# All of the first product by the seven-product scheme from the second block on, its last part moved behind the second product's first

## The chip, the core and the metric

The kernel runs on one core of one Trainium2 chip. A core has five engines that run beside each other, each in the order of its own queue: TensorE (PE; its weight loads are shown as PEld), VectorE (DVE), ScalarE (ACT), GpSimd (POOL) and SyncE (SP), which only starts transfers here. The metric is the device time of one launch in microseconds (us), taken as the median of several runs.

## The reference

Two stages follow each other. The first is a decayed linear attention (retention) over 768 tokens, for 4 batches and 8 heads of width 64; the second is a two-layer feed-forward with a Mish activation.

```python
for t in range(S):                                  # S = 768
    state = gamma * state + outer(k[:, :, t], v[:, :, t])
    y[:, :, t] = (1 / sqrt(64)) * q[:, :, t] @ state
x = y.transpose(0, 2, 1, 3).reshape(3072, 512)
h = x @ w_in                                        # 512 x 2048
g = h * tanh(softplus(h))                           # Mish
out = g @ w_out                                     # 2048 x 512
```

## The kernel before

The 3072 tokens are cut into 24 chunks of 128, and these into 11 blocks: block 0 has four chunks, blocks 1 to 10 have two each. For a block, the attention gives `xt` (the block's tokens of x, turned, FP16), the first product gives `g` through Mish, and the second product gives 256 rows of the output. In each block the attention of the next block runs in between: `scores` (queries by keys of a chunk), `mask` on VectorE, `y_two` (the attention's output for two chunks, and `outer_two`, the state's increments), then the copy to `xt`.

In a block after block 0 the second product (`seven`) is computed by the Strassen-Winograd scheme: the matrices are cut in 2 by 2 parts, and seven half-size products take the place of eight, at the price of sums before and after. Eight matmuls of 128x256 make one such product. The sums of `g` are written to `gsum` (s1 and s2 by `sums_a`, s3 by `sums_b`, s4 by `sums_c`), those of the weights to `tmat` once at the start (`weight_sums`).

The first product (`g1_seven`) is split before the change. The columns of w_in come as four slices of 512. Slices 0 and 2 go by seven products of eight 128x128 matmuls (`mm`, line 671), with `win_sums` giving the weight sums `wsum` and `x_sums` the token sums `xsum`. Slices 1 and 3 go plainly (`plain`, line 695): four pieces of eight 128x256 matmuls, each read straight from PSUM by a Mish on ScalarE (line 702). In the seven-product half three partial results are copied out of PSUM by ScalarE (`snap`, line 678), three sums PSUM + copy are formed by VectorE (`plus`, line 688), and four Mish follow (line 682).

PSUM has eight banks here: four for `mm` tiles of one bank (pool `mmps`), and two tiles of two banks each (pool `atps`, tag "at") that scores, `y_two` and the state increments share. A tile that needs a bank waits until the last reader of its earlier tenant is done.

The order is written out by hand: every engine executes its instructions in the order in which the code issues them, and the dictionaries of `steps_of` and `steps_of_first` say which work of the attention, the sums and the transfers is issued between which products. `gate(x)` is a one-element copy on GpSimd that makes GpSimd's queue wait for x. `sum_next` adds a state increment on VectorE, `decay_next` scales the state on GpSimd. Block 1 (`FIRST`) has its own dictionary; it also finishes block 0 (`last_ended`). In block 0, `cast_win` and `cast_wout` turn the loaded weights to FP16, and the list `late` holds sums of weights that `some_late` takes off one by one.

Of the kernel before, what the change touches and what calls it, by code (L numbers as in the profile page):

```python
# [16 lines left out]
def kernel(  # L17
# [165 lines left out]
    def cast_win(s, half, eng):  # L183
        src = wtmps["in", s]
        t = cpool.tile([P, NBP, TB // 2], FP16, name=f"win{s}_{half}")
        eng.tensor_copy(t, src[:, :, half * (TB // 2):(half + 1) * (TB // 2)])
        wins[s, half] = t
# [429 lines left out]
    def win_sums():  # L617
        wsums.append(wstage.tile([P, 4, NBP // 2, TB], FP16, name="wsum", tag="wt", bufs=4))
        sub, n = ALU.subtract, NBP // 2
        todo = []  # L620
        for half in range(2):
            s1, s2, s3, s4 = [
                wsums[0][:, i, :, half * (TB // 2):(half + 1) * (TB // 2)] for i in range(4)]
            a11, a12 = wins[0, half][:, :n], wins[0, half][:, n:]
            a21, a22 = wins[2, half][:, :n], wins[2, half][:, n:]
# [23 lines left out]
    def g1_seven(blk, steps):  # L649
# [4 lines left out]
        pb, px, pe = [mmps.tile([P, FPS, P], FP32, name="h_ps", tag="mm") for _ in range(3)]  # L654

        def a(i, j):
            return lambda f, d: win(2 * i, f, j * n + d)

        def s(i):
            return lambda f, d: wsums[0][:, i - 1, d, f * P:(f + 1) * P]  # L660

        def b(i, j):
# [5 lines left out]
        def mm(h_ps, w, x, first=False):  # L668
            for f in range(FPS):
                for d in range(n):  # L670
                    nc.tensor.matmul(  # L671
                        h_ps[:, f], w(f, d), x(d), start=first and f == 0 and d == 0,
                        stop=d == n - 1, skip_group_check=True)

        def snap(h_ps):
            x = hsnaps[0][:, nsnap[0] % 4].rearrange("p (f t) -> p f t", t=P)
            nsnap[0] += 1
            nc.scalar.copy(x, h_ps)  # L678
            return x

        def mish_of(i, j, h):
            nc.scalar.activation(  # L682
                gt[:, 2 * i * FPS:(2 * i + 1) * FPS, j * P:(j + 1) * P], h, AF.Mish,
                scale=inv_boost3)
# [6 lines left out]
        def plain(s, half):  # L691
            h_ps = mmps.tile([P, 2, 2 * P], FP32, name="h_ps", tag="mm")
            for j in range(2):
                for bp in range(NBP):
                    nc.tensor.matmul(  # L695
                        h_ps[:, j], win(s, 2 * half + j, bp), xt(blk, bp),
                        start=bp == 0, stop=bp == NBP - 1)
            return h_ps

        def mish_plain(s, half, h_ps):  # L700
            fb = s * FPS + 2 * half
            nc.scalar.activation(gt[:, fb:fb + 2], h_ps, AF.Mish, scale=inv_boost3)  # L702

# [494 lines left out]
```

## Time and profile before

| what | value |
|---|---|
| median of 3 runs | 198.35 us (197.97 to 198.6) |
| span of the profiled execution | 196.9 us, from its first to its last instruction |
| PE busy in the span | 190.0 us (97%) |
| DVE busy | 141.6 us (72%) |
| ACT busy | 105.5 us (54%) |
| POOL busy | 93.1 us (47%) |
| granted TensorE clock | 0.996 |
| the profiled execution's own time | not given beside its span |

The times of runs are those of whole executions; the profile gives of its own execution the span, and no other time. Between span and median lie 1.45 us, which are taken as what lies around the span. Rows of the chain and of the timeline give a start and a duration in us from the span's start. Matmuls are pipelined: in a row of several the last one's end is included, so that eight matmuls of 128x256 show as 1.04 us in the timeline but take 0.87 us of the chain.

### The profile page before, as it was taken

How to read it: one execution, taken by the hardware profiler on the slowest of the kernel's cores; microseconds unless marked ns; L12 is line 12 of the kernel's file. 1: busy time of each engine (PE TensorE's matmuls, PEld its weight loads, DVE VectorE, ACT ScalarE, POOL GpSimd, SP SyncE). 2: the span in 40 equal slices, each digit the busy share in tenths (PEclk: the TensorE clock that was granted, in tenths of full speed). 3: DMA queues.
4: the chain of work that ended last, by engine and by line, in shares of the span. 5: the costliest groups of instructions: out<-in, count | busy, mean ns of one | idle time of the engine just before them, and what ended most of it. 6: DMA issues, size and time to landing. Idle time of an engine off the chain costs nothing.

```text
span 196.9 us, 5965 instructions
## 1 busy us (share of the span) xinstructions
PE 190.0 (97%) x2482; PEld 158.8 (81%) x2482; DVE 141.6 (72%) x304; ACT 105.5 (54%) x193; POOL 93.1 (47%) x130
## 2 busy tenths in 40 slices
PE   6999999999999999999999999999999999999992
PEld 2557646876888988988988988988988988988991
DVE  3688699795897596597498596597497596596462
ACT  3364667443753753753753753753853843843930
POOL 4270214694848829918716818728626723110000
PEclk9999999999999999999999999999999999999998
DMA  5999999999999999997997994995988933101102
GB/s 170 350 375 405 405 407 225 331 174 83 137 214 237 232 205 230 197 130 199 179 212 97 227 172 103 153 217 119 176 201 128 189 65 110 55 0 72 41 27 80
DMA packets 95802, 36.06 MB, mean 183 GB/s; under 512 B 82592, under 2 KB 89376, under 8 KB 95776
## 3 DMA queue, kind: packets, MB, share of 16 engines
q1 hardware_dynamic: 74544, 33.04, 65.1%
q0 software_dynamic: 21088, 2.62, 22.3%
q8 instruction: 19, 0.31, 0.6%
q10 hardware_dynamic: 144, 0.03, 0.1%
q14 instruction: 7, 0.06, 0.1%
HBM read 27.30 MB, written 6.29 MB: 171 GB/s over the span
## 4 chain that ended last, share of the span: by engine, by line
PE 92%; DVE 2%; ACT 2%; issue 1%; POOL 0%; POOLq 0%; ACTq 0%
PE o_ps L777 32%; PE h_ps L695 17%; PE h_ps L671 15%; PE h_ps L556 5%; PE o_ps L1009 5%; PE y_ps L508 3%; PE at L439 3%; PE at L415 2%; PE o_ps L1067 2%; PE h_ps L866 2%; PE y_ps L499 1%; DVE am L291 1%; PE u_ps L454 1%; DVE st L315 1%; ACT hsnap L678 1%
## 5 line engine op out<-in xcount | busy, mean ns | idle before, releaser
L695 PE MATMUL h_ps<-xt,win 128*128 128x256 f16 x320 | 41.6, 273 | 0.0
L688 DVE TENSOR_TENSOR hsum<-h_ps,hsnap 128x512 f32<-128x512 f32 x30 | 19.8, 688 | 21.2 <-PE h_ps L671 19.1
L777 PEld LDWEIGHTS <-gsum 128*128 128x128 f16 x336 | 30.8, 98 | 4.1
L695 PEld LDWEIGHTS <-win 128*128 128x128 f16 x320 | 29.3, 98 | 3.6
L777 PE MATMUL o_ps<-tmat,gsum 128*128 128x256 f16 (+1 forms) x256 | 27.9, 266 | 0.0
L384 POOL DMA_DIRECT2D qk<-in_k_dram x36 | 27.8, 776 | 0.0
L777 PEld LDWEIGHTS <-g 128*128 128x128 f16 x256 | 23.7, 98 | 2.6
L682 ACT ACTIVATE g<-hsum 128x512 f16<-128x512 f32 x30 | 18.6, 630 | 11.7 <-DVE hsum L688 11.7
L445 DVE TENSOR_TENSOR am<-at,tri 128x1024 f16<-128x1024 f32 x20 | 24.2, 1216 | 0.2 <-PE at L439 0.2
L702 ACT ACTIVATE g<-h_ps 128x512 f16<-128x512 f32 x40 | 22.7, 599 | 2.4 <-PE h_ps L695 2.4
L397 POOL COPY gate<-gsum 128x1 f16<-128x1 f16 x12 | 2.6, 213 | 44.3 <-DVE gsum L743 36.8
L786 ACT COPY snap<-o_ps 128x256 f32<-128x256 f32 (+1 forms) x32 | 11.4, 359 | 21.7 <-PE o_ps L777 21.5
L389 POOL TENSOR_TENSOR v<-vf,qvs 128x512 f16<-128x512 f32 x20 | 23.0, 1153 | 0.0
L678 ACT COPY hsnap<-h_ps 128x512 f32<-128x512 f32 x30 | 16.4, 580 | 12.1 <-PE h_ps L671 12.1
L799 DVE TENSOR_TENSOR osb<-o_ps,snap 128x256 f32<-128x256 f32 (+1 forms) x31 | 12.7, 410 | 12.6 <-PE o_ps L777 11.5
L372 POOL TENSOR_TENSOR qk<-qf,qvs 128x512 f16<-128x512 f32 x20 | 21.7, 1086 | 0.0
L541 ACT CAST xt<-y_ps 128x1024 f16<-128x1024 f32 x10 | 10.1, 1012 | 19.3 <-PE y_ps L499 14.3
L671 PEld LDWEIGHTS <-wsum 128*128 128x128 f16 x320 | 19.6, 98 | 0.8 <-issue 0.3
L777 PE MATMUL o_ps<-wout,g 128*128 128x256 f16 (+1 forms) x168 | 19.3, 268 | 0.0
L671 PE MATMUL h_ps<-xsum,wsum 128*128 128x128 f16 x240 | 16.7, 219 | 0.2 <-ACT hsnap L678 0.2
L671 PEld LDWEIGHTS <-win 128*128 128x128 f16 x240 | 15.1, 98 | 0.7
L614 DVE TENSOR_TENSOR gsum<-g 128x256 f16<-128x256 f16 (+1 forms) x30 | 9.9, 331 | 3.8 <-ACT g L682 3.6
(126 smaller groups left out, 296.1 us busy)
## 6 DMA issues: line engine op xcount, KB each, us to landing
vf<-in_v_dram SPq DMA_DIRECT2D x24, 256.0 KB, 5.3
out_dram<-osb SPq DMA_DIRECT2D x22, 256.0 KB, 4.7
qf<-in_q_dram SPq DMA_DIRECT2D x20, 256.0 KB, 4.3
wi<-in_moe_w_in_dram SPq DMA_DIRECT2D x3, 1024.0 KB, 10.6
wt<-in_moe_w_out_dram SPq DMA_DIRECT2D x3, 1024.0 KB, 8.8
qk<-in_k_dram POOLq DMA_DIRECT2D x36, 64.0 KB, 4.4
qfirst<-in_q_dram SPq DMA_DIRECT2D x2, 512.0 KB, 4.4
kf<-in_k_dram SPq DMA_DIRECT2D x4, 256.0 KB, 5.0
```

Of the source, the lines that this page charges most:

```text
L372: nc.gpsimd.tensor_tensor(by_head(g, room16(g)[0]), by_head(0, loaded[g][0]), f.broadcast_to((P, 2, HP, D)), op=ALU.mult)
L384: nc.gpsimd.dma_start(room16(g)[1][:, x::2], src[:, HP * x:HP * x + HP])
L389: nc.gpsimd.tensor_tensor(room16(g)[2], loaded[g][2], vs.unsqueeze(2).broadcast_to((P, H, D)), op=ALU.mult)
L445: nc.vector.tensor_tensor(am, ats.pop(g), tri.unsqueeze(1).unsqueeze(1).broadcast_to((P, 2, HP, C)), op=ALU.mult)
L671: nc.tensor.matmul(h_ps[:, f], w(f, d), x(d), start=first and f == 0 and d == 0, stop=d == n - 1, skip_group_check=True)
L678: nc.scalar.copy(x, h_ps)
L682: nc.scalar.activation(gt[:, 2 * i * FPS:(2 * i + 1) * FPS, j * P:(j + 1) * P], h, AF.Mish, scale=inv_boost3)
L688: nc.vector.tensor_tensor(h, h_ps, x, op=ALU.add)
L695: nc.tensor.matmul(h_ps[:, j], win(s, 2 * half + j, bp), xt(blk, bp), start=bp == 0, stop=bp == NBP - 1)
L702: nc.scalar.activation(gt[:, fb:fb + 2], h_ps, AF.Mish, scale=inv_boost3)
L777: nc.tensor.matmul(t, x(f), w(f)[:, c], start=first and f == 0, stop=f == n - 1, skip_group_check=True)
L799: nc.vector.tensor_tensor(dst[:, c], t, plus[:, c], op=ALU.add)
```

## The change

`g1_seven` computes slices 1 and 3 by seven products as well. There are now two groups, g = 0 (slices 0 and 2) and g = 1 (slices 1 and 3), each of seven products of eight 128x128 matmuls; `plain` is gone. Group 1 has weight sums of its own (`win_sums(1)`, eight more VectorE operations in block 0). The cast of slice 3 of w_in moves from VectorE to ScalarE in block 0. Of the fourteen products of a block, thirteen stand in `g1_seven`; the last one of group 1 (`rest`) stands in `seven`, behind the second product's first product and the scores. A two-bank "at" tile (`both`) holds two of the eight PSUM tiles that the two groups need. One of the six copies out of PSUM, that of the fifth product of group 0, is made by VectorE. The sums of `g` are issued later: s1 and s2 in two parts of the size 128x512 (before: one of this size and two of 128x256), s3 behind the first mask and s4 behind the second. In `seven`, the products with `sm(1)` and `sm(2)` now come ahead of the one with `wouts` that completes the first. GpSimd's second gate of a block (`gate_s`, which waits for s4) stands in blocks 2 to 8 too, ahead of the casts of q and v and the loads of k that the block issues there; before it stood in block 1 alone. The remaining weight sums of w_out are made before block 1, not in it.

```diff
@@ cast_win
-        eng.tensor_copy(t, src[:, :, half * (TB // 2):(half + 1) * (TB // 2)])
+        src = src[:, :, half * (TB // 2):(half + 1) * (TB // 2)]
+        if eng is nc.scalar:
+            nc.scalar.copy(t, src)
+        else:
+            eng.tensor_copy(t, src)
...
@@ win_sums
-    def win_sums():
-        wsums.append(wstage.tile([P, 4, NBP // 2, TB], FP16, name="wsum", tag="wt", bufs=4))
+    def win_sums(a):
+        if a == 0:
+            t = wstage.tile([P, 4, n, TB], FP16, name="wsum", tag="wt", bufs=4)
+            wsums.append([t[:, i] for i in range(4)])
+        else:
+            wsums.append([
+                lpool.tile([P, n, TB], FP16, name="wsum", tag="kf", bufs=4) for _ in range(4)])
...
@@ g1_seven
-        pb, px, pe = [mmps.tile([P, FPS, P], FP32, name="h_ps", tag="mm") for _ in range(3)]
+        both = atps.tile([P, 2, FPS, P], FP32, name="h_ps", tag="at")
+        pb, px, pe, px1 = [
+            mmps.tile([P, FPS, P], FP32, name="h_ps", tag="mm") for _ in range(4)]
+        pb, px, pe = [pb, both[:, 0]], [px, px1], [pe, both[:, 1]]
...
-        mm(px, a(0, 0), b(0, 0), True)
-        m1 = snap(px)
-        step("p1")
-        mm(pb, a(0, 1), b(1, 0), True)
-        c11 = plus(pb, m1)
-        step("p2")
-        h0 = plain(1, 0)
-        mm(px, s(2), t(2))
-        mish_of(0, 0, c11)
-        u2 = snap(px)
-        mm(pe, s(1), t(1), True)
-        m5 = snap(pe)
-        mish_plain(1, 0, h0)
-        step("p6")
-        h1 = plain(3, 0)
...
+        def first_two(g):
+            mm(px, g, w(0, 0), x(0, 0), True)
+            m1[g] = snap(px[g])
+            mm(pb, g, w(0, 1), x(1, 0), True)
+        def second(g):
+            mm(px, g, s(2), t(2))
+            u2[g] = snap(px[g])
+        def fifth(g):
+            mm(pe, g, s(1), t(1), True)
+            m5[g] = snap(pe[g], g == 0)
+        first_two(0)
+        step("g1")
+        c0 = plus(pb[0], m1[0])
+        first_two(1)
+        mish_of(0, 0, 0, c0)
+        step("g2")
+        c1 = plus(pb[1], m1[1])
+        second(0)
+        mish_of(1, 0, 0, c1)
+        fifth(0)
+        step("g3")
+        second(1)
+        fifth(1)
+        mm(px, 0, s(3), t(3))
+        c22 = plus(px[0], m5[0])
+        mm(pe, 0, s(4), x(1, 1))
+        c12 = plus(pe[0], u2[0])
+        mish_of(0, 1, 1, c22)
+        mish_of(0, 0, 1, c12)
+        step("g4")
...
+        step("g5")
+        mm(px, 0, w(1, 1), t(4))
+        mish_of(0, 1, 0, px[0])
+        def rest():
+            mm(px, 1, w(1, 1), t(4))
+            mish_of(1, 1, 0, px[1])
@@ seven
-        pb, pe = [mmps.tile([P, hf], FP32, name="o_ps", tag="mm") for _ in range(2)]
         px = [mmps.tile([P, wide], FP32, name="o_ps", tag="mm") for _ in range(parts)]
+        pe = mmps.tile([P, hf], FP32, name="o_ps", tag="mm")
...
         mm(px, a(0, 0), b(0, 0), True)
         m1 = snap(px)
+        step("g7")
         step("m1")
+        rest()
+        pb = mmps.tile([P, hf], FP32, name="o_ps", tag="mm")
+        mm(pe, s(1), tm(1), True)
+        m5 = snap(pe)
+        step("m5")
+        mm(px, s(2), tm(2))
+        u2 = snap(px)
+        step("m6")
         mm(pb, a(0, 1), b(1, 0), True)
...
@@ first_block
-        late.extend(weight_sums(0) + weight_sums(1))
-        plan = {9: [(cast_wout, 0), (room_for_more,), (bring_first,)],
+        def more_sums():
+            late.extend(win_sums(1))
+            some_late(8)
+            late.extend(weight_sums(0) + weight_sums(1))
+        plan = {6: [(cast_win, NSL - 1, 0, nc.scalar)],
+                7: [(cast_win, NSL - 1, 1, nc.scalar), (more_sums,)],
+                9: [(cast_wout, 0), (room_for_more,), (bring_first,)],
@@ steps_of
+            "g1": [*then((gate_x, blk), (cast_q, a)), (sum_next, a - 3), (decay_next, a - 3),
+                   (cast_v, a), (bring_k, a + 1)],
+            "g2": [(store_due, 1), (turn_and_load, a)],
+            "g3": [(store_due, 2), (sum_next, a - 2)],
+            "g5": [(store_due, 3), (sums_a, blk, A)],
+            "g7": [(sums_a, blk, B)],
+            "m1": only((scores, a - 2), (scores, a - 1), (mask, a - 2)),
+            "m5": [(sums_b, blk), *only((gate_g, blk), (decay_next, a - 2))],
+            "m6": [*only((mask, a - 1)), (sums_c, blk), *then((gate_s, blk)),
+                   (cast_q, a + 1), (cast_v, a + 1), (bring_k, a + 2)],
+            "m2": [(turn_and_load, a + 1)],
...
@@ steps_of_first
-            "p1": [(last_ended.pop(),)],
-            "p2": [(gate_x, blk), (cast_q, a - 1), (bring_k, a), (sum_next, a - 2)],
+            "g1": [(last_ended.pop(),), (gate_x, blk), (cast_q, a - 1), (bring_k, a), (sum_next, a - 2)],
...
```

Three places show how the instructions stand now. The first is VectorE in block 0, from the last casts of slice 2 of w_in to the second slice of w_out; before (`win` and `wout` are cast weights, `wi` and `wt` the loaded ones, `wsum` the sums for the first product, `gsum` and `tmat` those for the second):

```order
L633 TENSOR_TENSOR wsum<-win_0_381,wsum 128x2x256
L186 COPY win_0_534<-wi 128x1024
L186 COPY win_1_536<-wi 128x1024
L633 TENSOR_TENSOR wsum<-win_1_527 128x2x256
L633 TENSOR_TENSOR wsum<-wsum,win_1_458 128x2x256
L633 TENSOR_TENSOR wsum<-win_1_458,win_1_527 128x2x256
L633 TENSOR_TENSOR wsum<-win_1_458,wsum 128x2x256
L194 COPY wout_574<-wt 128x2048
L591 TENSOR_TENSOR tmat<-wout_574 128x1024
L976 TENSOR_TENSOR gsum<-g 128x1024
L978 TENSOR_TENSOR gsum<-gsum,g 128x1024
L194 COPY wout_605<-wt 128x2048
```

The same place now, from the last sum of group 0's weights on:

```order
L643 TENSOR_TENSOR wsum<-win_1_458,wsum 128x2x256
L643 TENSOR_TENSOR wsum<-win_0_551 128x2x256
L643 TENSOR_TENSOR wsum<-wsum,win_0_499 128x2x256
L643 TENSOR_TENSOR wsum<-win_0_499,win_0_551 128x2x256
L643 TENSOR_TENSOR wsum<-win_0_499,wsum 128x2x256
L643 TENSOR_TENSOR wsum<-win_1_559 128x2x256
L643 TENSOR_TENSOR wsum<-wsum,win_1_501 128x2x256
L643 TENSOR_TENSOR wsum<-win_1_501,win_1_559 128x2x256
L643 TENSOR_TENSOR wsum<-win_1_501,wsum 128x2x256
L198 COPY wout_586<-wt 128x2048
L595 TENSOR_TENSOR tmat<-wout_586 128x1024
L1005 TENSOR_TENSOR gsum<-g 128x1024
```

Two casts of 128x1024 are gone from VectorE's queue there, and eight sums have come in ahead of the casts of w_out.

The second place is VectorE in a block in the middle, from the first sum PSUM + copy to the first mask; before:

```order
L688 TENSOR_TENSOR hsum<-h_ps,hsnap 128x512
L466 TENSOR_TENSOR suc<-u_ps,stc 128x256
L688 TENSOR_TENSOR hsum<-h_ps,hsnap 128x512 x2
L466 TENSOR_TENSOR suc<-u_ps,stc 128x256
L614 TENSOR_TENSOR gsum<-g 128x512
L615 TENSOR_TENSOR gsum<-gsum,g 128x512
L614 TENSOR_TENSOR gsum<-g 128x256
L615 TENSOR_TENSOR gsum<-gsum,g 128x256
L445 TENSOR_TENSOR am<-at,tri 128x1024
```

The same place now:

```order
L470 TENSOR_TENSOR suc<-u_ps,stc 128x256
L705 TENSOR_TENSOR hsum<-h_ps,hsnap 128x512 x2
L693 COPY hsnap<-h_ps 128x512
L470 TENSOR_TENSOR suc<-u_ps,stc 128x256
L705 TENSOR_TENSOR hsum<-h_ps,hsnap 128x512 x4
L618 TENSOR_TENSOR gsum<-g 128x512
L619 TENSOR_TENSOR gsum<-gsum,g 128x512
L618 TENSOR_TENSOR gsum<-g 128x512
L619 TENSOR_TENSOR gsum<-gsum,g 128x512
L449 TENSOR_TENSOR am<-at,tri 128x1024
```

Six sums and a copy out of PSUM stand where three sums stood, four of the six in one row, and all of s1 and s2 is ahead of the first mask.

The third place is ScalarE in the last block, from the copies of the first product to the last copy of the second; before:

```order
L678 COPY hsnap<-h_ps 128x512 x2
L702 ACTIVATE g<-h_ps 128x512 x2
L682 ACTIVATE g<-hsum 128x4x128 x2
L702 ACTIVATE g<-h_ps 128x512
L682 ACTIVATE g<-h_ps 128x4x128
L702 ACTIVATE g<-h_ps 128x512
L786 COPY snap<-o_ps 128x128 x4
L786 COPY snap<-o_ps 128x256
```

The same place now:

```order
L695 COPY hsnap<-h_ps 128x512 x2
L700 ACTIVATE g<-hsum 128x4x128 x4
L700 ACTIVATE g<-h_ps 128x4x128
L807 COPY snap<-o_ps 128x128 x2
L700 ACTIVATE g<-h_ps 128x4x128
L807 COPY snap<-o_ps 128x256
L807 COPY snap<-o_ps 128x128 x2
```

Four Mish that read sums of VectorE stand in a row ahead of the Mish that reads PSUM directly; in this block alone the second product's `px` has two tiles, and the tile `pe` gets the bank that this fifth Mish reads.

More of the change, by code (lines that the diff above doesn't have):

```diff
@@ L666, in t, with mm @@
             return lambda d: tsums[blk][:, i - 1, d]
-        def mm(h_ps, w, x, first=False):
+        def mm(h_ps, g, w, x, first=False):
             for f in range(FPS):
@@ L689, in plus @@
             return h
[L691 to L702, printed above, removed]
         def step(name):
@@ L941, in first_block @@
             mish(0, u, h_ps[u])
-        for s in range(1, NSL):
+        for s in range(1, NSL - 1):
             for half in range(2):
```

109 lines of the change are left out of this document (44 added, 65 removed).

## The prediction

> **What bounds the kernel now.** I read the page's shares first, then the chain of work that ended last, then the stretches of the blocks, and last the timeline of single blocks.
>
> ```profile
> span 196.9 us, 5965 instructions
> PE 190.0 (97%) x2482; PEld 158.8 (81%) x2482; DVE 141.6 (72%) x304; ACT 105.5 (54%) x193; POOL 93.1 (47%) x130
> PE 92%; DVE 2%; ACT 2%; issue 1%; POOL 0%; POOLq 0%; ACTq 0%
> ```
>
> PE is busy for 97% and is 92% of the chain. The busy time of matmuls says little by itself, since they overlap; that PE is the bound is seen from the chain, whose pieces in a block follow each other at the matmuls' own pace:
>
> ```profile
> 78.20 0.89 PE h_ps L671 x16
> 79.10 0.87 PE h_ps L695 x8
> ...
> 83.95 0.56 PE at L439 x16
> 84.50 0.98 PE h_ps L695 x8
> 85.48 4.37 PE o_ps L777 x40
> ...
> 90.89 1.85 PE o_ps L777 x16
> ```
>
> Here nothing but PE stands for a whole block: 16 matmuls of 128x128 take 0.89 (55.8 ns each), eight of 128x256 take 0.87 (109 ns), the five products of `seven` 4.37; `y_two` lies between 89.85 (85.48 + 4.37) and 90.89. The product behind the scores takes 0.98, 0.11 over its 0.87. The stretches, cut at the blocks' first matmuls, give the same per block, with VectorE's busy time as the fourth figure after the range:
>
> ```profile
> 48.40:63.38 14.98, 14.82 (x202) 13.03 (x201) 12.73 (x27) 8.41 (x17) 10.00 (x16) 1.00 1.22 183
> 63.38:78.04 14.66, 14.66 (x210) 13.13 (x208) 10.55 (x25) 8.08 (x15) 9.85 (x14) 1.00 1.26 226
> ...
> 165.63:180.05 14.42, 14.42 (x195) 12.85 (x193) 10.29 (x24) 8.09 (x15) 1.36 (x3) 1.00 0.11 39
> 180.05:192.90 12.85, 12.85 (x178) 12.16 (x175) 7.76 (x20) 7.07 (x16) 0.00 (x0) 1.00 0.17 62
> ```
>
> Blocks 2 to 9 are 116.67 from first to last (63.38 to 180.05), 14.58 each, with PE busy throughout. So fewer PE columns shorten the kernel at once, as long as VectorE (10.55 of 14.66) and ScalarE (8.08) keep up.
>
> **The change, part by part. PE's work.** A block loses 32 matmuls of 128x256 (32 x 109 ns = 3.49) and gains 56 of 128x128 (56 x 55.8 ns = 3.12): 0.36 less. Ten blocks: -3.6. The other products, scores and `y_two` stay in number. The pace of 55.8 ns is shown for 16 in a row; the new row has 104. In the rows of 16 each weight load starts with the matmul ahead of it, and nothing in them runs dry, so I take the same pace.
>
> The Trainium skill, TensorE: Matmul & The Clock Gate, section Back-to-back issue gap, speaks against that: it gives about 81 ns per matmul for a sustained stream of loads and matmuls at 128 columns. By that figure the 56 would take an estimated 4.5 and ten blocks about 10 more than now. This case's 0.89 for 16 disagrees with it.
>
> **Block 1 to 10, does the cover hold?** I lay out one middle block from the first matmul's issue (78.04) as time 0, with durations from these rows:
>
> ```profile
> 78.04 1.06 PE L671 MATMUL h_ps<-xt,win 128*128 128x128 f16 x16
> ...
> 78.69 0.58 ACT L678 COPY hsnap<-h_ps 128x512 f32<-128x512 f32 x1 [1.27 <-PE h_ps L671]
> ...
> 79.31 0.69 DVE L688 TENSOR_TENSOR hsum<-h_ps,hsnap 128x512 f32<-128x512 f32 x1 [0.25 <-ACT hsnap L678]
> ...
> 80.57 1.05 ACT L678 COPY hsnap<-h_ps 128x512 f32<-128x512 f32 x2
> ...
> 82.29 1.29 DVE L688 TENSOR_TENSOR hsum<-h_ps,hsnap 128x512 f32<-128x512 f32 x2 [1.96 <-PE h_ps L671]
> ...
> 83.02 1.23 ACT L682 ACTIVATE g<-hsum 128x512 f16<-128x512 f32 x2 [0.41 <-DVE hsum L688]
> ...
> 84.28 0.43 DVE L614 TENSOR_TENSOR gsum<-g 128x512 f16<-128x512 f16 x1 [0.36 <-ACT g L682]
> ...
> 84.74 0.43 DVE L615 TENSOR_TENSOR gsum<-gsum,g 128x512 f16<-128x512 f16 x1
> ...
> 88.21 1.21 DVE L445 TENSOR_TENSOR am<-at,tri 128x1024 f16<-128x1024 f32 x1
> ...
> 89.34 1.05 DVE L747 TENSOR_TENSOR gsum<-g,gsum 128x1024 f16<-128x1024 f16 x1
> ```
>
> A product of eight takes 0.45 of issue; its reader starts 0.20 after (78.49 to 78.69). One behind the other, a sum on VectorE costs 0.60 (1.29 - 0.69), a Mish on ScalarE 0.60 (1.23 - 0.63 of a single one), a copy 0.47, a mask 1.13 (88.21 to 89.34). The copy that moves to VectorE has no row; between 0.42 (half the size) and 0.69 (a sum of its size) I take 0.69. The ninth product ends its issue at 4.01. From 4.21 on VectorE forms four sums in a row, the last ending at 4.21 + 3 x 0.60 + 0.69 = 6.70. Four products more, the first of `seven` (0.87) and the first chunk's scores (0.28) bring PE to 6.94, where the second chunk's scores need the two-bank tile that the last of these sums reads: 0.2 to spare. On ScalarE the last of four Mish ends at 4.93 + 3 x 0.60 + 0.63 = 7.36; s1 of group 1 is then ready at 7.83, and PE wants it at 8.2 (6.94 + 0.28 of scores + 0.11 + 0.45 of the last product + half of the next 0.87). Mask, s3, mask, s4 follow from 8.2 on (1.13 + 0.60 + 1.13 + 1.05) to 12.2; PE wants s4 at 12.4 (7.78 + four products of 0.87 + 1.15 of `y_two` with the 0.11). All other waits (ScalarE's copies, the tile of two banks ahead of the eighth product) come out with 0.2 to 0.4 to spare. So in blocks 2 to 9 I take the new waits at nothing: the cover is 0.2, and each 0.1 beyond it costs 0.8 over eight blocks. VectorE gets three sums and a copy more, about 2.4, and is busy some 13.0 of 14.2. Bounds: 0 to 0.3 a block, 0 to 2.4 in all. A gain beyond PE's columns has no room, since PE has no gap there to lose.
>
> **Block 0: VectorE is late for w_out.** These rows set it:
>
> ```profile
> 24.40 0.42 DVE L633 TENSOR_TENSOR wsum<-win 128x512 f16<-128x512 f16 x1
> ...
> 24.45 0.60 ACT L572 ACTIVATE g<-h_ps 128x512 f16<-128x512 f32 x1 [0.27 <-PE h_ps L556]
> ...
> 25.94 1.29 DVE L186 CAST win<-wi 128x1024 f16<-128x1024 f32 x2
> 27.15 0.42 DVE L633 TENSOR_TENSOR wsum<-win 128x512 f16<-128x512 f16 x1
> ...
> 28.61 1.22 DVE L194 CAST wout<-wt 128x2048 f16<-128x2048 f32 x1
> ...
> 31.80 1.22 DVE L194 CAST wout<-wt 128x2048 f16<-128x2048 f32 x1
> ...
> 33.77 3.66 PE L1009 MATMUL o_ps<-wout,g 128*128 128x256 f16 x32
> ```
>
> Four weight sums take 1.54 (24.40 to 25.94) or 1.46 (27.15 to 28.61). Now four such groups stand in a row and the two casts (1.21) are gone: 24.40 + 1.54 + 3 x 1.46 = 30.32 for the first cast of w_out in place of 28.61. The second one, 3.19 + 1.22 behind, ends at 34.73 and not 33.02. PE wants that slice at 33.77 and has no idle time there: it waits 34.73 + 0.05 - 33.77 = 1.0. Bounds: 0 if the waits ahead of the sums leave more room than I see, 1.7 if the whole delay falls on PE. ScalarE's two casts (1.05 each, the row below) fit between its Mish, which come every 0.87 (0.60 and 0.27 of waiting, in the row of 24.45):
>
> ```profile
> L196 ACT CAST wout<-wt x3: 1045/1048/1048, 34.2 to 41.1; 128x1024 f16<-128x1024 f32 x3
> ```
>
> They put one Mish about 1.4 late (two casts less twice the 0.27). With four banks PE comes back to a bank 3 x 0.87 - 0.20 = 2.4 after the Mish on it could begin; 1.4 + 0.6 is less, so PE loses nothing there. The three weight sums that move from block 1 to its front, and the copy of turned q and k there that ScalarE takes over from VectorE, stand where these engines wait for PE: nothing, and if that cover is gone, the 0.6 of one sum.
>
> **Block 1.** Its VectorE begins late, since it still ends block 0:
>
> ```profile
> 50.00 0.42 DVE L1076 TENSOR_TENSOR osb<-o_ps,osb 128x256 f32<-128x256 f32 x1
> ...
> 50.93 0.42 DVE L463 TENSOR_TENSOR stc<-u_ps,gcv 128x256 f16<-128x256 f32 x1
> ...
> 51.07 1.03 PE L695 MATMUL h_ps<-xt,win 128*128 128x256 f16 x8
> ...
> 52.27 0.61 PE L671 MATMUL h_ps<-xsum,wsum 128*128 128x128 f16 x8 [0.16 <-ACT hsnap L678]
> ```
>
> Before, PE lost 0.33 here (51.07 + 8 x 0.109 = 51.94, and the next starts at 52.27). Now the two small operations come at 1.60 and 1.94 after the block's start (48.40), the first sum at 2.28 and not 1.27, and the second ends at 3.57. The eighth product writes the tile that this sum reads and waits from 3.12 to 3.6; the copies behind it add 0.25: 0.74 in all, 0.41 more than before. Bounds: -0.33 to 0.9.
>
> **Block 10.** Its second product uses two tiles for `px`, and so `pe` gets the bank of group 0's last product, whose Mish stands behind four others on ScalarE: 4.93 + 4 x 0.60 + 0.59 = 7.92. There are no scores in this block, and PE is there at 5.79 + 16 x 0.0558 + 0.45 = 7.13: it waits 0.83. Bounds 0 to 0.9.
>
> **The sum** against the profiled execution: -3.63 + 1.0 + 0.41 + 0.83 = -1.4, so a span of 195.5. SP's queue I cost at nothing: its transposes wait for the k loads, which now end 1 to 2 later in the block, and the loads of q and v stand behind them, but the scores read a transpose a block later (14.2), against
>
> ```profile
> qkt<-qk SPq DMA_TRANSPOSE x18, 3.9
> ```
>
> 3.9 to its landing.
>
> The median lies 1.45 above the span; I keep that and get 197.0.
>
> **Rivals.** *VectorE's queue sets the block's length* (slower). Its cover is only 0.2. If the four sums ran one after the other without overlap (0.69 each), or came late, every 0.17 a block beyond the cover takes up the whole gain; at 0.5 a block the time is 201. For it: 13.0 busy of 14.2, strictly in order. Against it: the two sums in 1.29 overlap already. *GpSimd is late.* The new gate starts two casts, two k loads, then the next block's gate, a cast and the state's scaling only when s4 is done (12.2), by
>
> ```profile
> L384 POOL DMA_DIRECT2D qk<-in_k_dram x36 | 27.8, 776 | 0.0
> L389 POOL TENSOR_TENSOR v<-vf,qvs 128x512 f16<-128x512 f32 x20 | 23.0, 1153 | 0.0
> L372 POOL TENSOR_TENSOR qk<-qf,qvs 128x512 f16<-128x512 f32 x20 | 21.7, 1086 | 0.0
> ...
> 80.47 0.61 POOL L471 TENSOR_TENSOR stc<-suc,gcv 128x256 f16<-128x256 f32 x1 [0.32 <-PE h_ps L671]
> ```
>
> 1.09 + 1.15 + 1.55 + 1.09 + 0.61 and two gates of 0.2, 5.9 later: 3.9 in the next block of 14.2, where the state's second addition (0.33) has to be begun by 3.88 to leave the four sums at 4.21. It decides from there on; 0.2 a block late gives 198.6. Where POOL, which waits then, leaves VectorE's s4 alone, that could end earlier than its 1.05 here. *Block 0 loses nothing*: 196.0. *The long row runs at 81 ns*, the page's figure taken as a mechanism (weight loads fall behind in rows longer than 16): 56 x 0.081 - 3.49 = +1.05 a block, 207.5; nothing in the rows of 16 shows a beginning of it.
>
> **How the numbers follow.** The forecast, 197.0, has 0.48, with its own range 196.3 to 197.9; VectorE's queue 0.20 (198.4 to 201), GpSimd 0.14 (197.5 to 199), block 0 without a loss 0.12, the slow row 0.02, others 0.04. From 195.6 to 199.6 leaves out the upper half of the first rival, the slow row and a part of the others. A change under 0.3% (0.6 us) can't be told from none here: faster means below 197.8. That takes in nearly all of the forecast, block 0's case and a little of GpSimd's: 0.60; slower, above 198.9, VectorE's and the rest: 0.25; between them 0.15.
>
> **What would show it.** Right: blocks 2 to 9 take 14.2 each with PE without a gap over 0.1; one gap of about 1.0 ahead of the products with the second slice of w_out in block 0, with VectorE's cast of it as the releaser; about 0.7 lost in block 1; one gap of about 0.8 in block 10, released by a Mish. Wrong: gaps at the second chunk's scores or at `y_two` that repeat in each block (VectorE late), VectorE waiting for the state's scaling (GpSimd), or a pace over 56 ns in the row of 13 products.

## The result, and the profile after

The changed kernel takes 197.32 us (median of 5 runs, 197.13 to 197.6) against 198.33 of the kernel before (5 runs, 197.97 to 198.6): a ratio of 0.9955, 95% interval 0.9942 to 0.9969. It is faster, by about 1.0 us between the medians or 0.5%, and it lies 0.3 above the forecast of 197.0. The profiled executions differ by more, 196.9 to 195.3; where the difference between 1.6 and 1.0 comes from is told below.

The page of the changed kernel has these lines for the shares and for the chain that ended last:

```profile
span 195.3 us, 6554 instructions
PE 187.2 (96%) x2722; PEld 158.1 (81%) x2722; DVE 162.8 (83%) x329; ACT 118.7 (61%) x216; POOL 92.0 (47%) x135
PE 80%; DVE 13%; ACT 3%; issue 2%; POOL 0%; POOLq 0%; DVEq 0%
```

VectorE (DVE) went from 72% to 83% of the span. It now has 13% of the chain, where it had 2%. All of that lies before 53.4 us, in block 0 and the beginning of block 1, but for one sum PSUM + copy in block 10 and the last copy of all. A middle block is still TensorE (PE) alone, as the pieces of the chain show (start, duration in us, and how many matmuls):

```profile
79.18 5.81 PE h_ps L685 x104
84.99 0.87 PE o_ps L798 x8
...
86.97 3.49 PE o_ps L798 x32
91.50 1.85 PE o_ps L798 x16
```

The thirteen products of 128x128 matmuls stand in one row of 104 that takes 5.81: 55.9 ns each. The stretches between the blocks' first matmuls (length, then the busy time of PE, PEld, DVE, ACT and POOL, the granted clock, the DMA share and GB/s), for block 1, 2, 3, 10 and for blocks 2 to 9 as one:

```profile
49.48:64.72 15.24, 14.81 (x226) 13.12 (x225) 13.38 (x28) 9.79 (x19) 9.71 (x15) 1.00 1.12 186
64.72:79.02 14.30, 14.30 (x235) 13.05 (x233) 12.69 (x26) 9.19 (x17) 8.81 (x15) 1.00 1.52 220
79.02:93.19 14.17, 14.17 (x227) 12.93 (x225) 12.50 (x26) 9.18 (x17) 8.64 (x14) 1.00 0.95 172
178.38:191.80 13.42, 12.77 (x202) 12.23 (x199) 10.00 (x23) 8.32 (x18) 0.00 (x0) 1.00 0.16 60
64.72:178.38 113.66, 113.66 (x1811) 103.58 (x1809) 99.65 (x199) 73.19 (x136) 59.82 (x91) 1.00 0.92 157
```

The same eight blocks of the kernel before, in the same view:

```profile
63.38:180.05 116.67, 116.67 (x1619) 104.33 (x1617) 84.88 (x184) 64.68 (x120) 61.31 (x84) 1.00 0.87 153
```

Blocks 2 to 9 gain 116.67 - 113.66 = 3.01, or 0.38 each, and are 14.21 long on average. Block 1 is 1.03 longer than that. What TensorE waits for after 30 us is, by the list of waits (total, times, longest):

```profile
PE o_ps L1038 <- DVE wout L198: 0.8, 1, 0.8
PE o_ps L798 <- ACT g L700: 0.7, 1, 0.7
PE h_ps L685 <- ACT osb L1108: 0.3, 1, 0.3
```

These three stand in block 0, block 10 and block 1. The list counts from a matmul's modelled end. Counted against the matmuls' pace they are longer, as the timeline shows for the first two (the rows of block 0, then of block 10):

```profile
32.95 1.05 PE L1038 MATMUL o_ps<-tmat,gsum 128*128 128x256 f16 x8
33.54 1.22 DVE L198 CAST wout<-wt 128x2048 f16<-128x2048 f32 x1
34.82 3.67 PE L1038 MATMUL o_ps<-wout,g 128*128 128x256 f16 x32 [0.82 <-DVE wout L198]
...
185.08 0.61 PE L685 MATMUL h_ps<-xsum,win 128*128 128x128 f16 x8
185.71 0.58 ACT L700 ACTIVATE g<-h_ps 128x512 f16<-128x512 f32 x1
186.34 1.93 PE L798 MATMUL o_ps<-tmat,gsum 128*128 128x256 f16 x24 [0.65 <-ACT g L700]
```

Block 0: 32.95 + 8 x 0.109 = 33.82, and the next product starts at 34.82, 0.06 behind the end of VectorE's cast of slice 1 (33.54 + 1.22): 1.0 lost. Block 10: 185.08 + 8 x 0.0558 = 185.53, the next starts at 186.34: 0.81 lost, behind the fifth Mish. In block 1 the same view shows this:

```profile
45.87 1.07 DVE L596 TENSOR_TENSOR tmat<-wout,tmat 128x1024 f16<-128x1024 f16 x1
46.30 1.53 POOL L376 TENSOR_TENSOR qk<-qf,qvs 128x512 f16<-128x512 f32 x1
46.85 1.52 DVE L597 TENSOR_TENSOR tmat<-wout,wout 128x1024 f16<-128x1024 f16 x1
...
48.90 0.68 DVE L598 TENSOR_TENSOR tmat<-wout,tmat 128x1024 f16<-128x1024 f16 x1
...
49.48 0.61 PE L685 MATMUL h_ps<-xt,win 128*128 128x128 f16 x8
49.50 0.41 DVE L1106 TENSOR_TENSOR osb<-o_ps,osb 128x256 f32<-128x256 f32 x1
...
49.95 0.37 ACT L1108 COPY osb<-o_ps 128x256 f32<-128x256 f32 x1 [0.65 <-DVE osb L1106]
...
50.37 1.50 PE L685 MATMUL h_ps<-xt,win 128*128 128x128 f16 x24 [0.28 <-ACT osb L1108]
...
52.03 1.28 DVE L705 TENSOR_TENSOR hsum<-h_ps,hsnap 128x512 f32<-128x512 f32 x2
```

The block's second product could start at 49.48 + 8 x 0.0558 = 49.93 and starts at 50.37: 0.44 lost, on a bank that ScalarE's copy (L1108) reads behind VectorE's L1106. Both finish a piece of block 0's output, and L1106 comes late behind three weight sums. Two of these sums take 1.07 and 1.52 and the third 0.68, for the same size. The first sum of the two groups comes at 52.03, 2.55 after the block's start, and the rest of the 1.03 is lost further on.

### The profile page after: what moved, and what is told of

The parts are those of the page before. It is cut to its first block, busy times and chain, and to the rows that moved or that the text cites. A ratio compares the mean times of both kernels' runs of the same rounds, so it can differ in the third digit from the quotient of the medians.

```text
span 195.3 us, 6554 instructions
## 1 busy us (share of the span) xinstructions
PE 187.2 (96%) x2722; PEld 158.1 (81%) x2722; DVE 162.8 (83%) x329; ACT 118.7 (61%) x216; POOL 92.0 (47%) x135
## 4 chain that ended last, share of the span: by engine, by line
PE 80%; DVE 13%; ACT 3%; issue 2%; POOL 0%; POOLq 0%; DVEq 0%
PE o_ps L798 31%; PE h_ps L685 30%; PE o_ps L1038 4%; PE at L443 3%; DVE wsum L643 3%; PE y_ps L512 3%; PE at L419 2%; PE h_ps L889 2%; ACT g L700 1%; PE y_ps L503 1%; DVE am L449 1%; DVE wout L198 1%; DVE hsum L705 1%; DVE am L295 1%; PE u_ps L458 1%
## 5 line engine op out<-in xcount | busy, mean ns | idle before, releaser
L705 DVE TENSOR_TENSOR hsum<-h_ps,hsnap 128x512 f32<-128x512 f32 x60 | 38.5, 685 | 5.9 <-PE h_ps L685 3.3
L700 ACT ACTIVATE g<-hsum 128x512 f16<-128x512 f32 x60 | 36.9, 630 | 3.7 <-DVE hsum L705 3.6
L695 ACT COPY hsnap<-h_ps 128x512 f32<-128x512 f32 x50 | 28.0, 582 | 14.6 <-PE h_ps L685 14.6
L685 PEld LDWEIGHTS <-wsum 128*128 128x128 f16 x640 | 36.3, 98 | 0.5 <-issue 0.3
L685 PE MATMUL h_ps<-xsum,wsum 128*128 128x128 f16 x480 | 30.4, 219 | 0.1
L685 PEld LDWEIGHTS <-win 128*128 128x128 f16 x480 | 28.2, 98 | 1.8 <-issue 0.4
L685 PE MATMUL h_ps<-xt,win 128*128 128x128 f16 x320 | 19.7, 219 | 0.3 <-ACT osb L1108 0.3
L685 PE MATMUL h_ps<-xsum,win 128*128 128x128 f16 x160 | 12.3, 220 | 0.0
L685 PE MATMUL h_ps<-xt,wsum 128*128 128x128 f16 x160 | 12.2, 219 | 0.0
L700 ACT ACTIVATE g<-h_ps 128x512 f16<-128x512 f32 x20 | 11.9, 594 | 0.0
```

The lines of the kernel that those rows point to most:

```text
L685: nc.tensor.matmul(h_ps[g][:, f], w(g, f, d), x(d), start=first and f == 0 and d == 0, stop=d == n - 1, skip_group_check=True)
L700: nc.scalar.activation(gt[:, fb:fb + FPS, j * P:(j + 1) * P], h, AF.Mish, scale=inv_boost3)
L705: nc.vector.tensor_tensor(h, h_ps, x, op=ALU.add)
```

## The experiments

Theory at first: TensorE's columns give -3.6, and three waits take 2.5 of it back (1.0 in block 0, 0.8 in block 10, and 0.7 in block 1, where 1.03 is lost now and 0.33 was lost before). Times below are medians, and ratios are to runs of the kernel before that stand beside each experiment (198.42 to 198.53). The changed kernel's 197.32 stands against 198.33, a ratio of 0.9955. The time of an execution is longer than its span, in the changed kernel and in five experiments by 1.96 to 2.06, in the kernel before and in the other seven by 1.72 to 1.85, so where these two kinds meet the spans are compared.

**The cast of slice 1 of w_out earlier.**

```diff
-12: [(g_sum, 1), (g_sum, 2), (cast_wout, 1), (room_for_more,), (g_sum, 3)],
+12: [(g_sum, 1), (cast_wout, 1), (room_for_more,), (g_sum, 2), (g_sum, 3)],
```

> Block 0, VectorE's order alone: the cast of slice 1 of w_out stands ahead of the second sum of g (0.69 us, 0.60 to the next) instead of behind it. Theory (VectorE's queue is the cause of block 0's gap of 0.98 us on TensorE): the gap falls to 0.98 - 0.60 = 0.38, and since VectorE waits for TensorE (0.55) ahead of the masks of block 0, some 0.55 of it is kept: 197.32 - 0.55 = 196.8. Rival (VectorE's total work up to block 1 sets its end, whatever the order): the gap in block 0 shrinks but comes back at the second product of block 1 (0.44 now, 1.0 then): 197.3. Second rival (the transfer of slice 1 is late, not its cast): gap stays 0.98.

Measured: 197.40 (197.16 to 197.84), ratio 0.9947 [0.9934, 0.9961], not to be told from the changed kernel. The gap ahead of slice 1 fell to 0.26, so the queue was its cause. But 0.34 appeared one product earlier and 0.29 at the turn of q and k (their transposes on TensorE), and block 1's 0.44 became 0.70: the rival of VectorE's total work is nearer. The 0.34 has another source. In this run's timeline VectorE's cast of slice 0 starts while GpSimd is issuing loads, and takes longer:

```profile
29.82 2.58 POOL L385 DMA_DIRECT2D qk<-in_k_dram  x2
30.42 1.50 DVE L198 CAST wout<-wt 128x2048 f16<-128x2048 f32 x1
```

In the changed kernel's profiled execution the first issue begins 0.5 earlier, the cast starts between the two issues, and it is the pair of issues that takes longer:

```profile
29.29 2.76 POOL L385 DMA_DIRECT2D qk<-in_k_dram  x2
...
30.35 1.22 DVE L198 CAST wout<-wt 128x2048 f16<-128x2048 f32 x1
```

Of the nine profiled executions in which this cast stands there (the changed kernel's and those of eight experiments) it took 1.50 or 1.51 in five and 1.22 in four. In each of the five the list of waits has TensorE's wait for the first sum of `g` behind it, and in none of the four. The kernels are alike up to there, so these 0.3 us change from one profiled execution to the next.

**Another bank in block 10.**

```diff
-        pe = mmps.tile([P, hf], FP32, name="o_ps", tag="mm")
+        pe = (atps.tile([P, 2, hf], FP32, name="o_ps", tag="at")[:, 0] if last
+              else mmps.tile([P, hf], FP32, name="o_ps", tag="mm"))
```

> Block 10 alone: the tile of the product with s1 comes from the other pool of two-bank tiles, which has no scores in this block, and so waits for no Mish. Theory (TensorE's 0.76 us there is the bank of the last product of group 0, read by the fifth Mish): the first four matmuls start at once, the next four wait for the second half of s1 (it ends at 186.25 in the trace of after; TensorE wants it at 185.57 + 0.44): about 0.3 is left, -0.44, 196.9. Rival (s1 itself is what is late): the gap stays, moved by one matmul, 197.3. Second rival (the shared cause is ScalarE, and s3 and s4 come later in the same way): the gain is given back before the end, 197.3.

Measured: 197.14 (196.58 to 197.49), ratio 0.9928 [0.9911, 0.9945]; span 194.6. The product starts at once and waits in its middle, 0.35, no longer for a Mish but for the second half of s1:

```profile
PE o_ps L799 <- DVE gsum L618: 0.2, 1, 0.2
```

The 0.81 was the bank for 0.46, and the sums of `g` for the rest. The profiled execution is the fastest of the six; between the medians the gain is 0.18.

**The last weight sum back into block 1.**

```diff
-            if (p, i) == ends[0]:
-                some_late(1)
...
-                   (turn_by_dma, a + 1), (load_v, a + 2), (store, 2), (load_to, a + 4)],
+                   (turn_by_dma, a + 1), (load_v, a + 2), (store, 2), (load_to, a + 4),
+                   (some_late, 1)],
```

> The last of the weight sums of w_out goes from the end of block 0 back into block 1 (behind the completion of the first quarter of its second product). Theory: it delayed VectorE's reading of the first bank that block 1 needs, and so TensorE's second product there by 0.44; that gap goes, and the later ones of block 1 (0.58 together) shrink by 0.16: -0.6, 196.7. Rival (ScalarE is late by its cast of the block's input, 48.29 to 49.30): the gap stays. Second rival (VectorE has no room for 0.6 later in block 1 either, with 13.0 of 13.9 busy): a gap of up to 0.6 at the scores of block 2 or at y_two of block 1, 197.3.

Measured: 197.45 (197.24 to 197.8), ratio 0.9949 [0.9937, 0.9962]. The 0.44 went, as the theory had it, and the later gaps of block 1 stayed at 0.75 together. But block 2 became 14.77 long in place of 14.30: the second rival. How that came about is seen at the end of block 1 in this run's timeline:

```profile
62.52 0.68 DVE L598 TENSOR_TENSOR tmat<-wout,tmat 128x1024 f16<-128x1024 f16 x1
62.54 1.56 POOL L376 TENSOR_TENSOR qk<-qf,qvs 128x512 f16<-128x512 f32 x1
64.06 1.04 POOL L393 TENSOR_TENSOR v<-vf,qvs 128x512 f16<-128x512 f32 x1
64.28 0.97 DVE L654 TENSOR_TENSOR xsum<-xt 128x256 f16<-128x256 f16 x1
```

The moved sum ran into GpSimd's cast of q, which took 1.56 and not 1.04. The cast of v came later by that, and VectorE's next sum of x ran into it: 0.97, where the others of its size take 0.28.

**The three together.** The edits are the three diffs above.

> The three edits of e1, e2 and e3 together. Theory (three separate waits, each with its own cause): -0.55 - 0.44 - 0.6 = -1.6, 195.7. Where block 0 and block 1 share VectorE's queue as one cause, the first and third partly overlap: -1.2, 196.1. Rival (VectorE's total work is the bound): -0.4 at most, 196.9.

Measured: 196.87 (196.45 to 197.24), ratio 0.9917 [0.9902, 0.9932]: 0.45 under the changed kernel, near the rival's 196.9. Of the three edits only that of block 10 brings its gain to the end: block 3 begins at 79.11 here and at 79.02 in the changed kernel, so the other two have gained nothing by then.

**Without the eight weight sums of group 1.**

```diff
-            late.extend(win_sums(1))
-            some_late(8)
+            wsums.append(wsums[0])
             late.extend(weight_sums(0) + weight_sums(1))
```

> The eight weight sums of group 1 are left out (2.9 us of VectorE in block 0); group 1 takes those of group 0 in their place, so slices 1 and 3 are not computed as the reference has them, with the same matmuls. Theory (one backlog of VectorE, which these eight sums make, is behind both the 1.0 us that TensorE loses in block 0 and the 1.0 in block 1): both go, -2.0 against 197.32: 195.3. Rival (two causes: the queue of block 0, and in block 1 its own order of VectorE's work, with the end of block 0, the state and the sums of x ahead of the first sum): block 0's 1.0 goes and of block 1's only the 0.44: 195.9. Rival (the transfer of slice 1 is what is late): 197.

Measured: 196.10 (196.07 to 196.22), ratio 0.9878 [0.9864, 0.9891], span 194.3. Here group 1 takes group 0's weight sums in place of its own, so slices 1 and 3 are not the reference's. Block 0's gap is gone. Block 1's are not, and its first has grown from 0.44 to 0.70:

```profile
PE h_ps L685 <- ACT osb L1107: 0.5, 1, 0.5
```

So there is no single backlog. The eight sums make block 0's wait, and block 1's has a cause of its own. That cause lies behind the masks of block 0, since ahead of them VectorE still waits 0.29 for TensorE. The theory of one total fell here.

**Slice 2's cast wholly on ScalarE,** with the edit of block 10.

```diff
-        cast_wout(2, 2)
+        cast_wout(2, FPS)
```

> The edit of e2, and the cast of slice 2 of w_out wholly on ScalarE (VectorE gives away 0.69 us behind block 0's gap, ScalarE takes 1.05 more, from 35.35 to 36.4). Theory (backlog): block 0's gap stays 0.98, VectorE comes 0.6 earlier through the weight sums, and the 0.44 at the second product of block 1 goes: 0.4 to 0.6 under e2's 197.14, 196.6. Rival (VectorE waits for TensorE twice on the way, 0.87 and 0.55, and so has no backlog from block 0 to carry; what makes it late at block 1 lies behind that): 197.1, with VectorE's waits longer by 0.6. Rival (ScalarE's second cast is late for the products with slice 2, wanted at 36.56): a new gap, 197.2 or more.

Measured: 197.07 (196.83 to 197.25), ratio 0.9926 [0.9912, 0.9940]: no different from 197.14 without it, and the spans are no shorter (medians 195.3 and 195.2). VectorE has 0.69 less to do and waits for ScalarE's cast in its place:

```profile
36.23 0.69 DVE L596 TENSOR_TENSOR tmat<-wout,tmat 128x1024 f16<-128x1024 f16 x1 [0.97 <-ACT wout L200]
```

Block 1's first gap is 0.72. This too says that its cause comes later than this cast.

**One more sum on VectorE in blocks 2 to 9,** between the two pairs of sums, of 128x512 and then of 128x1024.

```diff
+    def one_more(blk):
+        t = hp.tile([P, 1, d_model], FP16, name="spare", tag="spare", bufs=1)
+        nc.vector.tensor_tensor(t, wouts[0][:, :1], wouts[0][:, 1:2], op=ALU.add)
...
+            "g4": only((one_more, blk)),
```

> One operation more on VectorE in blocks 2 to 9, between the two pairs of sums (a sum of 128x512 f16 that nobody reads, 0.34 to the next one). Theory (the second chunk's scores start 0.05 behind their releaser; they start 0.25 behind the fourth sum, so the cover is 0.20): 0.14 a block, gaps ahead of the ninth score matmul, span 195.3 + 8 x 0.14 = 196.4. Rival (VectorE's total counts, 13.0 of 14.2 busy, and it still waits 1.1 a block ahead of the next block's sums of x): no change, 195.3. Rival (the next cover, s1 of group 1, is less than 0.2): more than 0.14 a block.

> As before, but the sum has 128x1024 (0.60 to the next one). Theory: 0.60 - 0.20 = 0.40 a block, span 195.3 + 3.2 = 198.5. Rival (total): 195.3 still, since 13.0 + 0.6 is under 14.2. Rival (later covers run out as well, s4 above all, 0.2 on paper): above 198.5, with gaps at y_two or at the product with s4.

Measured, one run each: spans 196.9 and 199.4. Blocks 3 to 9 in the view of stretches, for the changed kernel, with the small and with the large sum:

```profile
79.02:178.38 99.36, 99.36 (x1579) 90.54 (x1577) 86.95 (x174) 64.00 (x119) 51.01 (x77) 1.00 0.83 148
```

```profile
79.53:179.97 100.44, 100.44 (x1578) 90.96 (x1576) 90.12 (x181) 64.41 (x119) 51.18 (x78) 1.00 0.88 148
```

```profile
80.19:182.50 102.31, 100.68 (x1579) 90.94 (x1577) 92.01 (x181) 64.48 (x119) 51.20 (x78) 1.00 0.82 143
```

1.08 / 7 = 0.15 a block for 0.34 more work, and 2.95 / 7 = 0.42 for 0.60. The cover (the room that VectorE has before TensorE waits) is 0.18 to 0.19, and beyond it each 0.1 costs 0.1 a block: the theory's 0.14 and 0.40, and not the rival of the total. With the large sum the wait has the place and the releaser that the prediction named:

```profile
PE at L443 <- DVE hsum L705: 2.7, 8, 1.0
```

Both spans are longer than expected (0.5 and 0.9). Block 1 begins at 49.42 and 49.44, no later than in the changed kernel, so block 0 adds nothing to this. Block 2 does, which grew by 0.57 and 1.20 where the theory had 0.14 and 0.40. With the small sum a sum of `g` (L618) takes 0.91 there beside GpSimd's cast of v, and not its 0.42; with the large one the added sum takes 1.47 beside that cast, and 0.68 in block 3.

**GpSimd's casts behind the weight sums.** By now the suspect for block 1 is the length of the sums themselves, 1.07 and 1.52 beside GpSimd's casts. In the four experiments where block 1's first gap is 0.70 to 0.72, the first of them takes 1.33 or 1.34 in place of 1.07. The last three stand in a row, and the casts wait for them:

```diff
-        some_late(2)
+        some_late(3)
+        gate(tmats[1][:, 1, FPS, :1])
...
-            if (p, i) == ends[0]:
-                some_late(1)
```

> At the end of block 0 the last three weight sums of w_out stand in a row ahead of block 0's own ends, and GpSimd's casts of v and q there (L393, L376) wait for the third of them, so that they no longer run beside the second and third. In the trace of after these sums of 128x1024 took 1.07 and 1.52 beside GpSimd's casts, and 0.68 where GpSimd stood still. Theory (VectorE is late in block 1 because sums with both inputs in SBUF stretch beside GpSimd): each takes 0.68 (0.60 to the next), VectorE's first sum of block 1 comes 1.1 earlier, the 0.44 and the 0.58 lost in block 1 go: -1.0, 196.3; half of it if the sums of x (L654 to L657) stretch in their place. Rival (the length of 1.5 is VectorE's own, or the other operand's): the sums take 1.5 again, 197.3. Rival (GpSimd's casts come 2 us later and with them the transposes of q and k for block 1's scores): a gap ahead of the scores of block 1, 197.3 or more.

Measured: 198.76 (198.42 to 199.31), ratio 1.0011 [0.9999, 1.0023], a miss in time. The timeline shows why, and that the sums have the length that the theory gave them:

```profile
45.59 0.68 DVE L596 TENSOR_TENSOR tmat<-wout,tmat 128x1024 f16<-128x1024 f16 x1
46.19 0.69 DVE L597 TENSOR_TENSOR tmat<-wout,wout 128x1024 f16<-128x1024 f16 x1
46.79 0.69 DVE L598 TENSOR_TENSOR tmat<-wout,tmat 128x1024 f16<-128x1024 f16 x1
...
47.74 1.04 POOL L393 TENSOR_TENSOR v<-vf,qvs 128x512 f16<-128x512 f32 x1
...
48.84 0.32 PE L458 MATMUL u_ps<-v,qk 128*64 128x64 f16 x8 [1.56 <-POOL v L393]
```

The three sums take 0.68 to 0.69 each, and the 0.44 in block 1 is gone. That alone doesn't show the sums as its cause, since TensorE comes to block 1 later here by more than they save: the outer products ahead of block 1 read the very v whose cast was held back, and TensorE loses 1.7 on it. None of the theories had that. The later gaps of block 1 are 0.75 here as well.

**The eight sums split.** Four of them stand behind the cast of slice 2 of w_out.

```diff
+    own = []
...
-            late.extend(win_sums(1))
-            some_late(8)
+            own.extend(win_sums(1))
+            for work in own[:4]:
+                work()
...
         cast_wout(2, 2)
+        for work in own[4:]:
+            work()
```

> Of group 1's eight weight sums four stand behind the cast of slice 2 of w_out in block 0, in place of ahead of the cast of slice 0 (1.46 us of VectorE). Theory: the cast of slice 1 ends at 33.3, TensorE wants it at 33.8, the gap of 0.98 goes, and no later product of block 0 waits (the sum L596 ends at 36.8, wanted at 37.3); of it some 0.3 comes back in block 1, as in e5 where the second product there lost 0.70 and not 0.44: 196.6. Rival (VectorE's total in block 0 sets it, wherever the sums stand): gaps of together 0.9 at other products of block 0, as in e1: 197.3.

Measured: 196.94 (196.63 to 196.97), ratio 0.9909 [0.9892, 0.9925], span 195.2. Slice 1 is there in time, but TensorE loses 0.64 at the turn of q and k, for GpSimd's cast of q, which waits for a weight sum (L596 in the changed kernel) that comes 0.13 earlier while TensorE is there 1.0 earlier:

```profile
PE t_ps L427 <- POOL qk L376: 0.5, 1, 0.5
```

Block 0 keeps 0.4 of the 1.0 (block 1 begins at 49.09 and not at 49.48), and block 1 takes 0.25 of it back (0.70 for 0.44). Of the 0.4 between the medians, 0.3 is time outside the span; the spans differ by 0.1.

**These two and the bank of block 10.** The edits are the two diffs above and that of block 10.

> The edits of e2, e9 and e10 together. Theory (three waits with causes of their own: the order of VectorE's work in block 0, its sums beside GpSimd at the end of block 0, a bank in block 10): -1.0 - 1.0 - 0.3 against 197.32: 195.0; block 0 and block 1 without gaps over 0.1. Rival (one total of VectorE's work over block 0 and block 1): the first two give no more than 1.0 together: 196.0.

Measured: 197.69 (197.48 to 198.06), ratio 0.9954 [0.9940, 0.9968], with the same loss of 1.7 for v.

**Only the cast of q waits.** As the last one, but the wait stands behind GpSimd's cast of v.

```diff
-        gate(tmats[1][:, 1, FPS, :1])
         for p in pairs:
             mm(px[p], a(p, 1, 2), t(4))
         cast_v(CPB + 2)
+        gate(tmats[1][:, 1, FPS, :1])
         cast_q(CPB + 2)
```

> As e11, but of GpSimd's two casts at the end of block 0 only that of q waits for the weight sums; that of v, for which the outer products ahead of block 1 waited 1.6 in e9, runs when it did in after. Theory: the 1.66 is gone, the first of the three sums still stretches beside the cast of v (1.07 to 1.33), the second and third take 0.68; TensorE's second product of block 1 waits no more; the later waits of block 1 stay at some 0.75, as in e9 and e3; block 0 loses 0.7 at the turn of q and k (for GpSimd's cast) as in e10, block 10 0.35. Against e10 (span 195.2, 196.94): -0.6 in block 1 and -0.3 in block 10: span 194.3, 196.0. Rival (the transposes for block 1's scores, now 2 us later on SP's queue, become the wait): a gap ahead of the scores of block 1, 196.9.

Measured: 195.67 (195.6 to 196.05), ratio 0.9858 [0.9839, 0.9877], span 193.9: faster than both kernels. VectorE's second and third weight sums take 0.68, and the first two products of block 1 stand in one row with the next two:

```profile
46.40 0.68 DVE L599 TENSOR_TENSOR tmat<-wout,wout 128x1024 f16<-128x1024 f16 x1
...
47.00 0.68 DVE L600 TENSOR_TENSOR tmat<-wout,tmat 128x1024 f16<-128x1024 f16 x1
...
48.76 1.95 PE L687 MATMUL h_ps<-xt,win 128*128 128x128 f16 x32
```

What is left of TensorE's waits:

```profile
PE t_ps L427 <- POOL qk L376: 0.5, 1, 0.5
PE h_ps L687 <- DVE hsum L707: 0.3, 1, 0.3
PE o_ps L801 <- DVE gsum L620: 0.2, 1, 0.2
```

The 0.44 is gone, with nothing in its place, and here TensorE comes to block 1 earlier than in the changed kernel (48.76 for 49.48). With the eight sums split and GpSimd's casts left as they were, the gap was 0.70. So it was the stretched sums that made it. The first sum still takes 1.34, beside the cast of v. Block 1 is 14.96 long and still loses 0.75; VectorE's L1113, ahead of the first sum PSUM + copy, waits 0.21 there for a copy on ScalarE (L1115), so VectorE's queue alone doesn't set this. The transpose behind the held cast starts 1.2 us later (49.02 for 47.85) and delays nothing. An earlier start of GpSimd's cast at the turn, and an order in block 1 that forms its first sum before the state's, were not tried.

## Why the prediction was right, and where not

*TensorE's work.* Foretold -0.36 a block from 55.8 ns in a row of 16; measured -0.38 a block and 55.9 ns in a row of 104. Right. By the 81 ns of the Trainium skill (TensorE: Matmul & The Clock Gate, Back-to-back issue gap) the row would have taken an estimated 8.4; the trace disagrees.

*The cover of 0.2 in blocks 2 to 9.* Right: the chain of these blocks has only TensorE's pieces, one behind the other, and the two runs with more VectorE work put the cover at 0.18 to 0.19, at the place named. The rival that gave VectorE's queue 0.20 was close: one more operation of 0.34 a block would have cost 0.15 a block. VectorE's added work was put too high, at 2.4 a block; by the stretches it is (99.65 - 84.88) / 8 = 1.85. GpSimd's second gate delayed nothing on TensorE's path.

*Block 0.* 1.0 foretold, 1.0 measured, with the releaser named; without the eight sums it is gone. Right.

*Block 10.* 0.83 foretold, 0.81 measured, with the fifth Mish as the releaser. Right; 0.35 of it stays with another bank, for the second half of s1.

*Block 1.* 0.74 foretold, 1.03 measured. The term itself, VectorE's first sum 2.28 after the block's start, is right: in the five runs in which the second product doesn't wait (the two with the sum back in block 1, and the three with GpSimd held back) that sum comes at 2.26 to 2.28, and block 1 loses 0.75. The step that failed is the price of "the three weight sums that move from block 1 to its front", which were to "stand where these engines wait for PE: nothing, and if that cover is gone, the 0.6 of one sum". VectorE had waited there before the change, ahead of two ends of block 0:

```profile
46.01 0.69 DVE L1073 TENSOR_TENSOR osb<-o_ps,osb 128x512 f32<-128x512 f32 x1 [1.07 <-PE o_ps L1067]
47.73 0.42 DVE L1076 TENSOR_TENSOR osb<-o_ps,osb 128x256 f32<-128x256 f32 x1 [1.03 <-PE o_ps L1067]
```

These 2.1 would have covered three sums of 0.60 each. But beside GpSimd's casts two of them took 1.07 and 1.52, and all three 3.0 in the chain (0.98, 1.45 and 0.60). That filled the waits and put L1106 late, which cost 0.44 at the second product; 0.3 of it is left in the end, since the later losses of block 1 fell from 0.75 to 0.59. The last experiment shows the cause: two of the sums back at 0.68, TensorE not delayed, and the 0.44 gone. The trace of before had such rows, a sum of 1.53 beside a cast of 1.50 and the s4 of 1.05 that the prediction shows; I did not ask why.

*The sum.* Span 195.5 foretold, 195.3 measured. By stretches, block 0 is 0.1 longer than the sum had it and block 1 0.2 longer (15.24, where 14.98 - 0.36 + 0.41 = 15.03), blocks 2 to 9 are 0.1 shorter, and 0.4 is gained where no term was. That last stands behind the last matmul: from its end to the end of the span it is 3.9 us before (196.9 - 193.0) and 3.5 after (195.3 - 191.8), and 3.5 to 3.6 in all twelve experiments. Nothing in the change touches this, and there is one trace of before only, so its cause stays open.

The 1.45 between span and median was too small. It set the median of some runs against the span of another. Where both are known of one execution, the kernel before takes 1.72 to 1.85 more than its span (44 runs beside the experiments) and the changed kernel 2.00 to 2.05 (five runs; 197.34 against 195.3 in the profiled one). This also tells where the 0.6 between 1.6 and 1.0 comes from: about 0.3 is time outside the span, which is longer in the changed kernel, and the rest is that the profiled execution of before, 198.6 to 198.8 by this, was slower than its median of 198.33. Why the time outside the span differs from kernel to kernel no run shows. The forecast's mechanism holds; its nearness to the measured time is in part luck, since a span 0.2 too long and an allowance 0.6 too short were off against each other.

## What to carry to other kernels

When work is moved to where an engine waits, read what runs beside it there and not only how long the wait is: here two of the three moved sums took 1.6 and 2.2 times as long and overran it. A wait that is removed shows the next one on another engine, so price the next two or three before moving anything, and above all what reads the result of whatever is held back. A cover worked out from the row of releases was good to 0.02 us, and one added operation of known size is a cheap way to test it.

## What the hardware showed that was not expected

VectorE's sums with both inputs in SBUF and GpSimd's casts hold each other up. A sum of 128x1024 takes 0.68 alone and 1.07 to 1.53 beside a GpSimd cast; the cast takes 1.04 alone and 1.53 or 1.56 when the sum is under way first. Masks that read PSUM were not stretched: two took 2.35 beside GpSimd's casts of v, where one alone takes 1.22 and a second adds 1.13. The Trainium skill, SBUF — State Buffer, Who interferes with whom, says that a VectorE instruction with two SBUF inputs contends with a GpSimd one that reads SBUF, that the pair of ports which they share is an exclusive lock, and that the order of issue decides which of the two is blocked. These rows agree, in both orders. The profile shows such blocking as a longer duration and not as a wait, so that no list of waits names it.

A cast from f32 to f16 in SBUF (128x2048) went from 1.22 to 1.50 when GpSimd was issuing loads as it started. Whether the cast started during an issue or between two changed from one profiled execution to the next, in kernels that are alike up to there.
